# Windowed attention into a gated convolution block on one core: thirteen convolutions summed on GpSimd, the first batch's loads split by sequence, the work in a new order

## The chip, the cores and the metric

The kernel runs on one core of a Trainium2 chip. The core has five engines that matter here, each with its own queue that is worked off strictly in order: TensorE (PE; its weight loads are listed as PEld), VectorE (DVE), ScalarE (ACT), GpSimd (POOL), and SyncE (SP), which in this kernel issues all DMAs but one. An instruction that waits for another engine's result holds up everything behind it in its own queue. The metric is the device time of one execution in microseconds.

## The reference

Two stages follow each other. The first is attention over a symmetric window of 32 positions either way, the second a two-layer block whose hidden values are gated by their own three-tap convolution along the sequence:

```python
# q, k, v: (8 batches, 8 heads, 576 positions, 64), float32
scores = q @ k^T / 8
scores = where(|i - j| <= 32, scores, -1e9)
attn = softmax(scores); x = attn @ v            # heads put side by side: (8, 576, 512)
h = relu(x @ w_in)                              # (8, 576, 1024)
conv[s] = conv_w[0]*h[s-1] + conv_w[1]*h[s] + conv_w[2]*h[s+1]   # per channel, zero at both ends
out = (h * sigmoid(conv)) @ w_out               # (8, 576, 512), float32
```

## The kernel before, in words

All matrix work is done in bfloat16 with float32 sums in PSUM. The program is a flat list of steps in the string `ORDER` (line 29); the loop at its end (line 597) takes word by word and issues the step's instructions, so a word's place fixes the place of its instructions in each engine's queue. `name,args@bank` names a step, its arguments, and the PSUM bank (of eight) that it writes first. Nothing is reordered afterwards.

**Attention**, for batch b and half G of the heads (four heads on 4 x 32 partitions): `lq`/`lk` load q or k (576 KB each) into one of six staging tiles `st`; `cq`/`ck` cast them to bfloat16 (`qb`), on GpSimd (`p`) or ScalarE (`a`); `tq`/`tk` transpose them on VectorE into `qT`/`kT`. `sc,b,G,h` multiplies windows of 128 keys with 64 queries; h says which part of the nine 64-query tiles (the first four, 1024 columns, or the last five, 1280). `ex` is the exponential on ScalarE, `mk` multiplies by the 0/1 window mask (VectorE, `d`), `av` multiplies with v, `nr` divides by the row sums. v is loaded (`lv`), cast (`cv`) and copied once more with a shift of 64 rows (`vo`); both copies hold a column of ones for the row sums. `xp`/`xe` (TensorE and ScalarE) or `xt` (a transposing DMA) put the result with channels on the partitions, in `xT`.

**The block** runs over 12 chunks of 384 rows. The first two are split in halves, so there are 14 pieces P (0 to 3 are halves), each with four pairs m2 of 128-channel groups: 56 pairs. `ph,P,m2` is the first projection, `re` its ReLU into `hT`, `pc`/`tp` the convolution, `th` the tanh, `ga` the gate into `gT` (sigmoid by tanh). `py,c,i` is the second projection of 128 rows of chunk c, `ye` copies it from PSUM into one of four tiles `y`, `st` stores it (256 KB). The letter of a pair says who does the convolution:

- `P`: TensorE with diagonal weights `diag_w` of 128x128, 2 x 3 matmuls; the tanh is one instruction.
- `A`, `D`: TensorE with 64x64 quarters, 12 matmuls. The second group comes out with its halves exchanged: with `A` two ScalarE tanh of 64 partitions turn them back through `z`, with `D` two VectorE gates of 64 partitions do.
- `X`: ScalarE writes the first tap into PSUM (2 instructions), VectorE adds the other two (4), and no TensorE is used.

`cw` brings `conv_w` by a small matmul into `conv_w_sb`, `dg,m` makes `diag_w` for a group, `li`/`ci` and `lo`/`co` load and cast the two weight matrices in four parts each. `s0` to `s7` fill constants and borders.

Of the kernel before, what the change touches and what calls it, by code (L numbers as in the profile page):

```python
# [14 lines left out]

ORDER = """
lq,0,1 s3 s1 lq,0,0 s2 cw@0 lv,0,1 s5 s0 s7 lk,0,1 dg,4,d lk,0,0 lv,0,2 dg,2,d lv,0,3 dg,1,d cq,0,1,a lv,0,0 dg,7,d  # L30
lv,0,4 dg,6,d dg,0,d li,0 cq,0,0,p tq,0,1 li,2 cv,0,1,p dg,5,d tq,0,0 li,3 ck,0,1,p s4 tk,0,1 li,1 ck,0,0,p dg,3,d
sc,0,1,0@0 lk,1,0 cv,0,2,p sc,0,1,1@4 tk,0,0 ex,0,1,0 vo,0,1,p lq,1,0 ex,0,1,1 mk,0,1,0,d sc,0,0,0@0 lq,1,1 ex,0,0,0
cv,0,0,p sc,0,0,1@4 mk,0,1,1,d cv,0,3,a vo,0,0,d lk,1,1 cv,0,4,p ex,0,0,1 mk,0,0,0,d av,0,1,0@0 nr,0,1,0 vo,0,2,p
av,0,0,0@2 lv,1,1 nr,0,0,0 vo,0,3,d ci,0,p xp,0,1@0 lv,1,2 xp,0,0@1 xe,0,1,a mk,0,0,1,d av,0,1,1@2 xe,0,0,a nr,0,1,1
av,0,0,1@4 lv,1,0 ci,2,p ph,0,0@0 nr,0,0,1 ci,3,p ph,0,2@6 re,0,0 lo,2 pc,0,0,P@7 re,0,2 ci,1,p xp,0,3@4 th,0,0,P
xp,0,4@5 lo,3 xe,0,3,a ph,0,3@6 ga,0,0,P ck,1,0,p xe,0,4,a xp,0,2@4 re,0,3 ph,0,1@7 xe,0,2,a lo,1 cq,1,0,p tk,1,0
pc,0,3,P@5 re,0,1 ph,1,3@4 th,0,3,P tq,1,0 lk,2,1 cq,1,1,p pc,0,1,P@6 re,1,3 ph,2,0@7 th,0,1,P ga,0,3,P sc,1,0,0@0
re,2,0 lo,0 ck,1,1,p tq,1,1 ph,2,2@4 ex,1,0,0 ph,1,0@5 ga,0,1,P re,2,2 lv,1,3 cv,1,1,p sc,1,0,1@0 mk,1,0,0,d re,1,0
ph,2,3@4 ex,1,0,1 tk,1,1 lv,1,4 cv,1,2,p pc,0,2,P@5 ph,2,1@6 re,2,3 vo,1,1,d th,0,2,P lk,2,0 cv,1,0,p sc,1,1,0@0
re,2,1 ph,1,2@4 ga,0,2,P ex,1,1,0 mk,1,0,1,d pc,1,0,P@5 lq,2,0 co,2,p re,1,2 mk,1,1,0,d ph,1,1@6 th,1,0,P pc,1,2,P@4  # L40
vo,1,0,d re,1,1 lq,2,1 co,3,p sc,1,1,1@0 th,1,2,P ga,1,0,P pc,1,3,P@6 ex,1,1,1 ga,1,2,P pc,1,1,P@5 lk,3,0 co,1,p s6
pc,2,1,P@4 th,1,3,P mk,1,1,1,d av,1,1,0@0 th,1,1,P av,1,0,0@2 th,2,1,P lv,2,1 ck,2,1,p ga,1,1,P pc,2,0,P@7 nr,1,0,0
pc,2,3,P@5 th,2,0,P nr,1,1,0 pc,2,2,P@2 lq,3,0 co,0,p tk,2,1 xp,1,1@3 xp,1,0@0 xe,1,1,a py,0,0@1 lv,2,0 cv,1,3,p
xe,1,0,a ga,1,3,P ga,2,0,P th,2,2,P lk,4,0 vo,1,2,d cv,1,4,a py,0,2@0 ye,0,0,a vo,1,3,d th,2,3,P lv,2,2 ck,2,0,p
ga,2,1,P ph,3,2@1 ga,2,3,P ye,0,2,a ga,2,2,P ph,3,0@3 st,0,0 cq,2,0,p re,3,2 tk,2,0 av,1,1,1@4 re,3,0 av,1,0,1@6
nr,1,1,1 lk,3,1 cq,2,1,p py,1,0@0 nr,1,0,1 lq,3,1 ck,3,0,p ph,3,3@4 tq,2,1 ye,1,0,a xp,1,2@1 lv,2,3 cv,2,1,p re,3,3
pc,3,2,P@0 tq,2,0 xe,1,2,a sc,2,1,0@2 th,3,2,P ph,3,1@6 ex,2,1,0 st,1,0 ga,3,2,P cq,3,0,p xp,1,3@1 tk,3,0 pc,3,0,P@7
re,3,1 xe,1,3,a xp,1,4@4 lv,2,4 cv,2,0,p pc,3,3,P@5 th,3,0,P mk,2,1,0,d pc,3,1,P@6 xe,1,4,a vo,2,0,d sc,2,1,1@0 st,0,2
ck,4,0,p th,3,1,P py,0,1@4 ex,2,1,1 ga,3,1,P ga,3,0,P lq,4,0 tq,3,0 th,3,3,P cv,2,2,p lq,4,1 sc,2,0,0@0 ye,0,1,a
ph,4,0@6 vo,2,1,p ga,3,3,P ex,2,0,0 tk,4,0 st,0,1 sc,2,0,1@0 ck,3,1,p re,4,0 ph,4,2@4 mk,2,1,1,d ex,2,0,1 lv,3,1  # L50
mk,2,0,0,d cq,3,1,p pc,4,0,P@6 tk,3,1 re,4,2 lk,4,1 cv,2,3,p av,2,0,0@0 lv,3,0 th,4,0,P mk,2,0,1,d vo,2,2,p av,2,1,0@2
py,1,1@4 ga,4,0,P lk,5,1 cv,2,4,p tq,3,1 lv,3,2 ph,4,3@6 vo,2,3,p ye,1,1,a nr,2,0,0 lq,5,0 pc,4,2,A@4 nr,2,1,0 re,4,3
cq,4,0,p av,2,1,1@0 th,4,2,A lv,3,4 pc,4,3,A@2 nr,2,1,1 cq,4,1,p av,2,0,1@6 xt,2,0 th,4,3,A ga,4,2,A ph,4,1@0 cv,3,1,p
xt,2,1 nr,2,0,1 re,4,1 ga,4,3,A sc,3,0,0@4 ck,4,1,p xt,2,2 pc,4,1,P@0 ex,3,0,0 tq,4,0 cv,3,0,p sc,3,1,0@2 th,4,1,P
lv,3,3 mk,3,0,0,d py,1,2@6 vo,3,0,p ex,3,1,0 ga,4,1,P xt,2,3 mk,3,1,0,d py,2,1@7 ye,1,2,a cv,3,2,p xt,2,4 vo,3,1,d
cq,5,0,p sc,3,0,1@0 ye,2,1,a lk,5,0 av,3,1,0@4 tk,4,1 ex,3,0,1 py,2,2@6 st,1,1 cv,3,4,p nr,3,1,0 lv,4,0 ck,5,1,p
mk,3,0,1,d lv,4,1 av,3,0,0@4 sc,3,1,1@0 st,2,1 nr,3,0,0 py,2,0@7 ex,3,1,1 tq,5,0 xt,3,1 cv,3,3,p tq,4,1 vo,3,2,p
sc,4,0,0@0 ye,2,0,a ph,5,0@4 ex,4,0,0 xt,3,0 vo,3,3,d ph,5,2@0 ck,5,0,p re,5,0 st,1,2 mk,4,0,0,d ye,2,2,a lq,6,0
mk,3,1,1,d ph,5,3@2 lq,5,1 re,5,2 tk,5,0 st,2,2 cv,4,0,p av,3,0,1@0 re,5,3 av,3,1,1@4 nr,3,0,1 lv,4,2 cv,4,1,p
pc,5,2,D@6 st,2,0 vo,4,0,p pc,5,0,A@2 nr,3,1,1 th,5,2,D lv,4,4 ph,5,1@0 th,5,0,A lv,4,3 ga,5,2,D xt,3,3 ph,6,2@4  # L60
# [573 lines left out]
```

## Time and profile before

| | before |
|---|---|
| three runs | 225.03, 223.29, 221.05 us (median 223.29) |
| span of the profiled execution (the page gives no other time for it) | 221.8 us |
| VectorE, ScalarE, GpSimd busy | 190.1, 162.3, 94.2 us |
| moved by DMA | 45.96 MB, 207 GB/s over the span |
| granted TensorE clock | 1.000 |

Times in a profile are counted from the span's start. Nearly every instruction is issued through one helper, so line numbers say little here and the groups are told apart by what they write and read: `gT<-PS,hT` is a gate, `qb<-st` a cast of q or k, `PS<-hT,diag_w` a convolution on TensorE. A group's row gives its form, how many there are, the busy time of them together (overlaps counted once), the mean of one in ns, and the engine's idle time just before them with what ended it.

### The profile page before, as it was taken

The numbers are of one execution on the slowest core, as the hardware profiler recorded it, in microseconds if no ns is written. First come the engines' busy times: TensorE is split into PE (matmuls) and PEld (weight loads), VectorE is DVE, ScalarE is ACT, GpSimd is POOL, SyncE is SP. The second block draws the span as 40 slices with busy tenths as digits, with TensorE's granted clock in tenths as the row PEclk, the third lists the DMA queues.
The fourth block names the chain that finished last, engine by engine and source line by source line (L and its number), as shares of the span: only waits on it lengthen the run. The fifth ranks groups of instructions, "written<-read, shape, count | busy, mean of one in ns | idle before, by whom it ended". The sixth has DMA issues, their size and how long they took to land.

```text
span 221.8 us, 7235 instructions
## 1 busy us (share of the span) xinstructions
PE 192.9 (87%) x3026; PEld 114.5 (52%) x3026; DVE 190.1 (86%) x321; ACT 162.3 (73%) x260; POOL 94.2 (42%) x113
## 2 busy tenths in 40 slices
PE   1044999799999899899998999999999999999993
PEld 0033898657754445554554554564555455554441
...
GB/s 214 333 263 386 339 254 351 354 318 350 284 313 300 137 133 258 250 260 193 369 332 178 222 230 244 222 53 106 98 3 145 69 136 50 38 79 42 142 101 136
DMA packets 65348, 45.96 MB, mean 207 GB/s; under 512 B 53516, under 2 KB 55588, under 8 KB 65316
## 3 DMA queue, kind: packets, MB, share of 16 engines
...
## 4 chain that ended last, share of the span: by engine, by line
PE 41%; DVE 40%; ACT 9%; issue 4%; POOL 3%; DMA 1%; ACTq 0%; DVEq 0%; POOLq 0%
PE PS L175 41%; DVE gT L175 9%; DVE attn L175 6%; DVE xn L175 6%; DVE kT L175 5%; DVE vo L175 5%; DVE qT L175 4%; ACT hT L175 3%; ACT z L175 3%; DVE diag_w L175 2%; ACT attn L175 2%; POOL qb L175 2%; DVE PS L175 2%; ACT PS L175 2%; DMA conv_w<-in_moe_conv_w_dram 1%
## 5 line engine op out<-in xcount | busy, mean ns | idle before, releaser
L175 PE MATMUL PS<-xT,w_in_sb 128*128 128x385 bf16 (+3 forms) x448 | 71.4, 309 | 1.2 <-DVE xn L175 0.5
L175 PE MATMUL PS<-w_out_sb,gT 128*128 128x512 bf16 x288 | 66.7, 380 | 0.1
L175 PEld LDWEIGHTS <-w_in_sb 128*128 128x128 bf16 x448 | 41.5, 100 | 25.7 <-issue 5.2
L175 POOL TENSOR_SCALAR qb<-st 128x1152 bf16<-128x1152 f32 x31 | 37.6, 1214 | 40.2 <-issue 8.9
L175 ACT ACTIVATE hT<-PS 128x770 bf16<-128x770 f32 (+3 forms) x56 | 40.2, 721 | 11.8 <-PE PS L175 10.8
L175 ACT ACTIVATE attn<-PS 128x1024 bf16<-128x1024 f32 (+1 forms) x32 | 36.0, 1132 | 11.2 <-PE PS L175 11.2
L175 DVE SCALAR_TENSOR_TENSOR gT<-PS,hT 128x384 bf16<-128x384 f32 (+2 forms) x66 | 40.2, 617 | 4.2 <-ACT PS L175 3.4
L175 PEld LDWEIGHTS <-gT 128*128 128x128 bf16 x288 | 26.5, 98 | 30.2 <-issue 0.9
L175 ACT ACTIVATE PS<-PS 128x384 f32<-128x384 f32 (+1 forms) x56 | 31.9, 572 | 6.2 <-PE PS L175 5.0
L175 POOL TENSOR_SCALAR ve<-vst 128x512 bf16<-128x512 f32 x38 | 28.4, 754 | 15.5 <-PE PS L175 11.6
L175 DVE TENSOR_TENSOR attn<-attn,mask 128x1024 bf16<-128x1024 bf16 (+1 forms) x32 | 29.3, 923 | 6.2 <-ACT attn L175 6.0
L175 ACT COPY y<-PS 128x512 f32<-128x512 f32 x36 | 20.8, 585 | 17.7 <-PE PS L175 17.7
L175 PE MATMUL PS<-hT,diag_w 64*64 64x384 bf16 (+2 forms) x456 | 31.1, 311 | 2.8 <-DVE gT L175 1.2
L175 DVE TENSOR_TENSOR xn<-PS,rec 128x512 bf16<-128x512 f32 (+1 forms) x32 | 26.4, 824 | 1.4 <-DVE rec L175 0.3
L175 PE MATMUL PS<-qT,kT 32*128 32x64 bf16 x1152 | 15.4, 195 | 11.7 <-DVE kT L175 9.3
L175 ACT ACTIVATE z<-PS 64x384 f32<-64x384 f32 x48 | 23.3, 485 | 0.9
L175 PEld LDWEIGHTS <-diag_w 64*64 64x64 bf16 (+1 forms) x456 | 18.3, 104 | 10.2 <-issue 6.3
L175 PEld LDWEIGHTS <-kT 32*128 32x128 bf16 x1152 | 11.9, 96 | 20.1 <-DVE kT L175 10.2
L175 DVE SCALAR_TENSOR_TENSOR PS<-hT,conv_w_sb,PS 128x384 f32<-128x384 bf16 x36 | 19.6, 618 | 1.6 <-ACT PS L175 1.6
L175 DVE STREAM_TRANSPOSE kT<-qb 128x576 uint32<-128x576 uint32 x16 | 19.7, 1240 | 0.7 <-PE PS L175 0.7
L175 PE MATMUL PS<-ve,attn 128*64 128x65 bf16 x384 | 16.4, 203 | 3.8 <-DVE attn L175 2.2
L175 DVE STREAM_TRANSPOSE qT<-qb 128x576 uint32<-128x576 uint32 x16 | 19.6, 1244 | 0.0
...
## 6 DMA issues: line engine op xcount, KB each, us to landing
...
```

The source lines that it names most:

```text
L175: return lambda *args, **kwargs: tc.keep_in_program_order(do(*args, **kwargs))
```

## The change

- **First batch.** For batch 0, q and k of both G are loaded, cast and transposed in two parts along the sequence (q: rows 0 to 255, 256 KB, and the rest; k: rows 0 to 287, 288 KB, and the rest). That makes four loads, four casts and four transposes more.
- **Kind `G`.** Thirteen pairs get a fifth kind. `add_tap` multiplies on GpSimd each of the two groups with its tap's weight (two instructions of 384 columns, 192 in a half piece) into a float32 tile, for the second and third tap into `tap`, and then adds `tap` to `zg` (one instruction of 768 columns): six multiplications and two additions. The tanh reads `zg` (two buffers) and writes the PSUM bank that the gate reads. Three of the thirteen are in half pieces.
- **Other kinds.** `A` goes from 24 pairs to 11, `D` from 5 to 7, `X` from 9 to 9 (one of them in a half piece now), `P` in whole pieces from 2 to 4 and in half pieces from 16 to 12.
- **Masks.** Eight of the 32 `mk` go to GpSimd: two `affine_select` of 64 partitions each that write zeros outside the window.
- **Who copies.** `cq`/`ck` on GpSimd: 31 whole ones become 21 and 4 of the parts; on ScalarE 1 becomes 7 and 4 parts. `cv` on ScalarE: 2 becomes 18. `ci`/`co` on ScalarE: none becomes 3. `dg`: 5 of 8 go from VectorE to ScalarE (three instructions of 128 columns each). `ye`: 10 of 36 go from ScalarE to VectorE.
- **End.** The last projection tile `py,11,2`, its copy and its store are done in two halves of 256 columns.
- **Order.** The whole string `ORDER` is another one, with other banks, and with it every queue: the first word is now a k load, loads of a batch stand in blocks, and two parts of `w_in` (`li,1`, `li,2`) are loaded behind q and k of batch 1 instead of before them. `cw` and the copy behind it (`cc`) are two words.

```diff
 ORDER = """
-lq,0,1 s3 s1 lq,0,0 s2 cw@0 lv,0,1 s5 s0 s7 lk,0,1 dg,4,d lk,0,0 lv,0,2 dg,2,d lv,0,3 dg,1,d cq,0,1,a lv,0,0 dg,7,d
-lv,0,4 dg,6,d dg,0,d li,0 cq,0,0,p tq,0,1 li,2 cv,0,1,p dg,5,d tq,0,0 li,3 ck,0,1,p s4 tk,0,1 li,1 ck,0,0,p dg,3,d
-sc,0,1,0@0 lk,1,0 cv,0,2,p sc,0,1,1@4 tk,0,0 ex,0,1,0 vo,0,1,p lq,1,0 ex,0,1,1 mk,0,1,0,d sc,0,0,0@0 lq,1,1 ex,0,0,0
...
-ga,13,3,A st,10,0 py,11,0@0 ye,10,2,a st,10,2 py,11,1@1 ye,11,0,a st,11,0 py,11,2@0 ye,11,1,a st,11,1 ye,11,2,a
-st,11,2
+lk,0,0,1 s1 cw@0 cc dg,6,a dg,0,d dg,3,a s4 lq,0,1,0 cq,0,1,0,p s2 s5 dg,7,d dg,2,a lk,0,1,0 ck,0,1,0,p s0 lq,0,0,0
+cq,0,0,0,a ck,0,0,1,a tk,0,1,0 lk,0,0,0 ck,0,0,0,p tq,0,0,0 tq,0,1,0 sc,0,1,0@0 lk,0,1,1 lv,0,2 ck,0,1,1,p cv,0,2,p
+ex,0,1,0 dg,1,a lq,0,1,1 lv,0,1 cv,0,1,p cq,0,1,1,a tk,0,0,0 s3 s7 sc,0,0,0@3 tk,0,0,1 tk,0,1,1 ex,0,0,0 lv,0,0
+cv,0,0,a mk,0,1,0,d tq,0,1,1 vo,0,1,d vo,0,0,d lq,0,0,1 sc,0,1,1@4 cq,0,0,1,a ex,0,1,1 tq,0,0,1 mk,0,0,0,p lv,0,4
+lv,0,3 cv,0,3,a li,0 li,3 lk,1,0 av,0,0,0@2 nr,0,0,0 av,0,1,0@0 sc,0,0,1@4 ex,0,0,1 nr,0,1,0 cv,0,4,p vo,0,3,d
+vo,0,2,d xp,0,0@2 xp,0,1@0 ci,0,a xe,0,0,a xe,0,1,a mk,0,1,1,p ck,1,0,p av,0,1,1@5 mk,0,0,1,d av,0,0,1@3 nr,0,1,1
...
+pc,13,3,X@2 ph,13,1@6 pc,12,2,G tp,12,2,G re,13,1 ph,13,0@4 re,13,0 th,12,2,G@6 py,8,2@0 tp,13,3,X ph,13,2@4 ye,8,2,a
+th,13,3,X re,13,2 ga,12,2,G py,10,1@6 st,9,0 st,8,0 ye,9,1,d ga,13,3,X pc,13,1,X@4 pc,13,2,A@1 ye,10,1,a tp,13,1,X
+py,9,2@0 py,10,0@7 pc,13,0,G tp,13,0,G py,10,2@6 st,8,2 st,9,1 th,13,2,A ga,13,2,A ye,9,2,a th,13,1,X th,13,0,G@1
+ga,13,1,X ye,10,0,a ye,10,2,a st,9,2 st,10,0 st,10,1 st,10,2 ga,13,0,G py,11,1@0 ye,11,1,a st,11,1 py,11,0@2 ye,11,0,a
+st,11,0 py,11,2,0@0 ye,11,2,0,a st,11,2,0 py,11,2,1@3 ye,11,2,1,a st,11,2,1
 """
+    zg_ = tiles(2, [128, 2, CH], FP32, "zg")
+    tap = tiles(1, [128, 2, CH], FP32, "tap")[0]
...
+    def part_of(y, part):
+        if not part:
+            return 0, RP
+        first = (256, 288)[y] // 32
+        return (0, first) if part[0] == 0 else (32 * first, RP - first)
...
     def mk(b, G, h, e):
         attn, n = attn_of(b, G, h)
-        {"d": vector, "p": gpsimd}[e].tensor_tensor(out=attn, in0=attn, in1=mask[:, 0:4 * n], op=ALU.mult)
+        if e == "d":
+            vector.tensor_tensor(out=attn, in0=attn, in1=mask[:, 0:4 * n], op=ALU.mult)
+            return
+        for lo, sign in ((0, 1), (64, -1)):
+            part = attn[lo:lo + 64].rearrange("p (t x) -> p t x", x=64)
+            gpsimd.affine_select(
+                out=part, in_=part, compare_op=ALU.is_ge, fill=0.0, base=0,
+                pattern=[[0, n // 16], [-sign, 64]], channel_multiplier=sign,
+            )
...
+    def add_tap(P, m2, kk):
+        z = where["zg", P, m2]
+        to = (tap if kk else z)[:, :, 0:width(P)]
+        for i in range(2):
+            m = 2 * m2 + i
+            gpsimd.tensor_scalar(
+                out=like(to[:, i, :], P), in0=taps(P, m, kk), scalar1=conv_w_sb[:, kk, m:m + 1],
+                scalar2=0.0, op0=ALU.mult, op1=ALU.add,
+            )
+        if kk:
+            z = z[:, :, 0:width(P)]
+            gpsimd.tensor_tensor(out=z, in0=z, in1=to, op=ALU.add)
...
+        if kind == "G":
+            where["pc", P, m2] = bank
+            scalar.activation(
+                conv_out(P, m2), where["zg", P, m2][:, :, 0:width(P)], AF.Tanh, bias=0.0, scale=1.0
+            )
+            return
```

194 lines of the change are left out of this document (110 added, 84 removed).

## The prediction

> **What bounds the kernel now.** First the span and busy times, then the same by stretch, then the chain of waits at both ends.
>
> ```profile
> span 221.8 us, 7235 instructions
> PE 192.9 (87%) x3026; PEld 114.5 (52%) x3026; DVE 190.1 (86%) x321; ACT 162.3 (73%) x260; POOL 94.2 (42%) x113
> ```
>
> ```profile
> core 0: us, PE busy (x) PEld busy (x) DVE busy (x) ACT busy (x) POOL busy (x), PEclk, DMA share, GB/s
> 0.00:24.48 24.48, 7.20 (x234) 5.99 (x234) 20.42 (x46) 8.22 (x9) 17.82 (x26) 1.00 1.01 310
> 24.48:75.00 50.52, 46.81 (x829) 34.78 (x829) 46.68 (x71) 36.28 (x65) 34.90 (x39) 1.00 1.08 305
> 75.00:120.00 45.00, 42.03 (x706) 22.94 (x698) 43.35 (x67) 35.21 (x55) 23.95 (x26) 1.00 1.02 243
> 120.00:160.00 40.00, 39.64 (x606) 20.78 (x604) 34.59 (x62) 32.51 (x51) 17.52 (x24) 1.00 0.73 171
> 160.00:200.00 40.00, 39.21 (x572) 21.71 (x571) 34.23 (x63) 35.91 (x57) 0.00 (x0) 1.00 0.30 76
> 200.00:222.00 22.00, 18.05 (x106) 8.28 (x104) 10.87 (x18) 14.21 (x25) 0.00 (x0) 0.99 0.26 99
> ```
>
> TensorE is idle 28.9 us: 17.3 before the first projection, 6.7 from there to 120 us, where VectorE has 90.0 of 95.5 us busy and is the bound, 1.1 to 200 us, where TensorE is the bound, and about 4 at the end. GpSimd does nothing after 160 us. The clock is full throughout and plays no part.
>
> ```profile
> 4.46 3.84 DVE diag_w L175 x6
> ...
> 13.16 0.64 PE PS L175 x29
> ...
> 200.29 17.82 PE PS L175 x104
> 218.13 0.58 ACT y L175
> ```
>
> In the chain of waits (start, length, what) the first scores come at 13.16 us, behind six `diag_w` on VectorE; the end is TensorE without a gap, then one copy and its store.
>
> **The start.** Loads and GpSimd's and TensorE's first work, from the timeline:
>
> ```profile
> 0.81 0.87 SPq L175 DMA_DIRECT2D st<-in_q_dram  x2
> 4.89 1.15 ACT L175 CAST qb<-st 128x1152 bf16<-128x1152 f32 x1 [2.16 <-DMA st<-in_q_dram]
> 6.55 1.35 POOL L175 TENSOR_SCALAR qb<-st 128x1152 bf16<-128x1152 f32 x1 [2.65 <-DMA st<-in_q_dram]
> 9.02 1.15 POOL L175 TENSOR_SCALAR qb<-st 128x1152 bf16<-128x1152 f32 x1 [0.24 <-DMA st<-in_k_dram]
> 11.74 0.62 POOL L175 TENSOR_SCALAR ve<-vst 128x512 bf16<-128x512 f32 x1
> 24.49 2.77 PE L175 MATMUL PS<-xT,w_in_sb 128*128 128x193 bf16 x16
> 85.92 4.09 PE L175 MATMUL PS<-xT,w_in_sb 128*128 128x385 bf16 x24
> 209.29 8.81 PE L175 MATMUL PS<-w_out_sb,gT 128*128 128x512 bf16 x40
> ```
>
> A 576 KB load takes 1.66 us of the stream (6.55 − 4.89) behind a fixed 2.4 us. The parts that the first scores need (third load in the queue) so land near 0.81 + 2.4 + 832/576 x 1.66 = 5.6 us; the GpSimd cast of a part, by 1152 and 512 columns (1.15 and 0.62 us) 0.65 us, ends at 6.3. VectorE has two `diag_w` (0.64 each) ahead of three part transposes instead of seven among whole ones. ScalarE makes three `diag_w` first and casts q's other part behind them, near 7.3 us, and VectorE transposes that part before the one needed. Scores: about 8.6 us, 4.5 earlier. From there ScalarE carries more than before: four exponentials, one `diag_w`, two part casts, two v casts, two `xe` and one weight cast, about 11 us by the rows below, against 11.3 us in the trace before (13.16 to 24.49). The next scores share bank 3 with the first and wait for their exponential (1.0 us); all of batch 0's later attention is queued behind on TensorE, and ScalarE fills the time with casts. First projection: near 20.3 us. I take −4.2. Bounds: 0, if the loads for it are late (below), and −4.5. The four more loads cost SyncE 0.43 us each (0.87 for two), hidden behind the transfers.
>
> **TensorE's share.** The groups by form:
>
> ```profile
> L175 PE MATMUL PS<-hT,diag_w 64*64 64x384 bf16 x348 | 18.8, 328 | 1.5 <-ACT hT L175 1.1 <-ACT PS L175 0.2
> L175 PE MATMUL PS<-hT,diag_w 128*128 128x192 bf16 x96 | 10.1, 246 | 1.3 <-DVE gT L175 1.2
> L175 PE MATMUL PS<-hT,diag_w 128*128 128x384 bf16 x12 | 2.3, 326 | 0.0
> L175 ACT ACTIVATE z<-PS 64x384 f32<-64x384 f32 x48 | 23.3, 485 | 0.9
> L175 ACT ACTIVATE PS<-PS 128x384 f32<-128x384 f32 x40 | 19.3, 482 | 3.7 <-PE PS L175 3.2
> L175 ACT ACTIVATE PS<-PS 128x768 f32<-128x768 f32 x16 | 12.8, 797 | 2.5 <-PE PS L175 1.8 <-DVE PS L175 0.4
> L175 ACT ACTIVATE PS<-hT,conv_w_sb 128x384 f32<-128x384 bf16 x18 | 9.7, 574 | 0.3
> L175 ACT COPY y<-PS 128x512 f32<-128x512 f32 x36 | 20.8, 585 | 17.7 <-PE PS L175 17.7
> L175 ACT CAST ve<-vst 128x512 bf16<-128x512 f32 x2 | 1.2, 624 | 0.0
> L175 DVE SCALAR_TENSOR_TENSOR gT<-PS,hT 128x384 bf16<-128x384 f32 x45 | 24.3, 549 | 3.4 <-ACT PS L175 3.1
> L175 DVE SCALAR_TENSOR_TENSOR gT<-z,hT 128x384 bf16<-128x384 f32 x24 | 16.4, 684 | 1.4 <-ACT z L175 1.2
> L175 DVE SCALAR_TENSOR_TENSOR gT<-PS,hT 128x768 bf16<-128x768 f32 x11 | 10.5, 952 | 0.6 <-ACT PS L175 0.3
> L175 DVE SCALAR_TENSOR_TENSOR gT<-PS,hT 64x384 bf16<-64x384 f32 x10 | 5.5, 555 | 0.2
> L175 DVE SCALAR_TENSOR_TENSOR PS<-hT,conv_w_sb,PS 128x384 f32<-128x384 bf16 x36 | 19.6, 618 | 1.6 <-ACT PS L175 1.6
> L175 POOL TENSOR_SCALAR qb<-st 128x1152 bf16<-128x1152 f32 x31 | 37.6, 1214 | 40.2 <-issue 8.9 <-DMA st<-in_q_dram 8.6 <-DVE qT L175 8.4
> L175 POOL TENSOR_SCALAR ve<-vst 128x512 bf16<-128x512 f32 x38 | 28.4, 754 | 15.5 <-PE PS L175 11.6 <-DMA vst<-in_v_dram 3.5
> masks.py:199 POOL TENSOR_SCALAR_AFFINE_SELECT ident<-ident 128x128 bf16<-128x128 bf16 x1 | 0.3, 292 | 0.1
> ```
>
> An `A` or `D` pair costs TensorE only 18.8/29 = 0.65 us, a half `P` 10.1/16 = 0.63, a whole `P` 1.15. Eleven `A`/`D` and four half `P` fewer, two whole `P` more: −7.1 − 2.5 + 2.3 = −7.3 us. By piece, 4.7 of it lies in pieces 1 to 7, 2.6 in pieces 8 to 13. The first part runs where VectorE is the bound, so VectorE's sum decides there.
>
> **VectorE.** Gates and taps: an `A` costs 0.55 + 0.68, `D` 0.55 + 2 x 0.56, whole `P` and `G` 0.95, half `P` and `G` 0.55, `X` 4 x 0.62 + 0.95. −13 `A`, +2 `D`, +2 whole and −4 half `P`, +10 whole and +3 half `G`, one `X` into a half piece: −3 us. Five `diag_w` at 0.64: −3.2. Eight masks at about 0.9: −7.2. Ten copies of 512 columns from PSUM, scaled from the 384-column gate to some 0.7: +7; at 0.585, as on ScalarE, +6. Together −6, and most of that in the start and the last third: from the first projection to piece 7 only two masks leave and four copies come. Against it stands a wait on GpSimd, seen in one row at two times:
>
> ```profile
> L175 DVE TENSOR_TENSOR attn<-attn,mask 128x1024 bf16<-128x1024 bf16 x14 | 12.7, 909 | 3.5 <-ACT attn L175 3.4
> ...
> L175 DVE TENSOR_TENSOR attn<-attn,mask 128x1024 bf16<-128x1024 bf16 x2 | 1.4, 686 | 0.5 <-ACT attn L175 0.5
> ```
>
> The first is before 160 us, with GpSimd 59% busy (94.2/160), the second after, with GpSimd idle: 0.22 us more per instruction. With GpSimd 78% busy to the end it would be 0.3 on some 70 masks, shifted v copies and gates from `z`: +3 us or so over the kernel. I take −1 us for the stretch from the first projection to 120 us (from 0 to −4), and nothing for VectorE behind it.
>
> **ScalarE.** Pairs: −13 `A` (0.48 + 2 x 0.485), and the others by their tanh: −9. Casts: 6 whole (1.15), 4 parts (0.65), 16 of v (0.62), 3 of weights (about 1.05), 15 instructions of `diag_w` (0.27 by the slope from 384 to 768 columns): +27. Nine copies `y`, halves counted: −6. Sum +12, so 174 of about 214: hidden beside VectorE and TensorE, and at the start already counted. Without that cover it costs up to 12.
>
> **GpSimd.** The trace has no `G` pair and no large `affine_select`. A multiplication of 384 columns, by the slope above, is 0.51 us. The addition of 768 columns with two inputs lies between one such stream, 0.83, and two, 1.66; I take two, because it reads two float32 tiles. A whole pair is 6 x 0.51 + 2 x 1.66 = 6.4 us (4.7 to 7.8, the upper end by the mean of the v casts, 754, over their undisturbed 620), a half one 4.2. A mask, from 0.29 us for 128 columns with the same slope, is 2.1 to 2.5. So: +64 + 13 (pairs), +18 (masks), −9 (ten q/k casts, four parts back), −12 (16 v casts), −3 (weights), +1: 94 becomes 166. From piece 5 on it is nine pairs, 13 casts of q or k, 11 of v, ten shifted copies and five masks, about 107 us. Before, piece 5 to TensorE's end is 85.92 to 218.1 us; less 3, and less what must follow the last pair (three tiles at 1.76, tanh 0.8, gate 0.95) and what precedes the first, 120 us are there. It fits, with 13 to spare. Each tanh of a `G` pair sits in ScalarE's queue: if the sum is late, the copies `ye` behind it wait, and TensorE for their banks. For the last pair (13,0), TensorE has five tiles, one projection and one convolution, 5 x 1.76 + 1.36 + 0.65 = 10.8 us, as cover after the projection, and GpSimd 6.4 plus what is left of pair (12,2); I add +1 us.
>
> **The end.** The last tile's second half starts 0.9 us earlier relative to its store: copy and store of 128 KB instead of 256 KB behind the last matmul. −0.7 (0 to −1; the same eight weights are loaded twice).
>
> Sum: 221.8 − 4.2 − 1.0 − 2.6 + 1.0 − 0.7 = 214.3 against the profile's span, whose own time the page doesn't give; the median of the runs is 1.5 above the span, so **215.8 us**.
>
> **Rivals.**
> *GpSimd becomes the bound from piece 5 on.* Above 7.9 us a pair ((120 − 50)/9), the queue of sums is longer than TensorE's work, and each 0.1 us adds 0.9: at 8.5 us 221, at 9.5 us 230, slower than before. It decides from 7.9 us. For it: both engines already lengthen each other (909 to 686 above, 754 to 620), and `z` gates and masks would now meet GpSimd after 160 us too. Against: fewer such VectorE instructions (71 for 94), and 13 us of room. The Trainium skill (SBUF — State Buffer, section "Who interferes with whom") says that a VectorE instruction with two SBUF inputs and a GpSimd instruction that reads SBUF exclude one another for a whole instruction. The trace agrees as far as 909 against 686 ns go. By that rule this rival is the likelier the longer GpSimd's instructions get.
> *The earlier start is lost.* The DMA share is 1.01 to 1.08 up to 75 us; 4.2 us at 305 GB/s are 1.3 MB that would have to come sooner, or VectorE, 94% busy, doesn't take it up. 215.8 + 4.2 = 220. Against: part of the loads wait for free staging tiles, not for the stream.
> *The addition costs one stream and VectorE sheds its 4 us.* 215.8 − 1 − 3 − 1 = 210.8.
>
> **Chances.** The measurement tells 2% from no change: 218.8 to 227.8 us is "within". The forecast (212 to 218.8) 0.47, the cheap addition 0.08: faster 0.55. The lost start 0.16 and GpSimd's milder half 0.11: within 0.27. GpSimd above 9.2 us a pair: 0.18. The range for 8 in 10 goes from 209 (a little under the cheap case) to 227, leaving out the slow tail; the forecast's own range is 212 to 219.
>
> **What would show it.** First scores near 8.6 us and the first projection near 20.3 in the timeline; the `zg` additions at 1.66 us each, and GpSimd near 166 us; VectorE still over 90% from the first projection to piece 7; masks and `z` gates after 160 us over 0.8 us. I am wrong if ScalarE's tanh from `zg` waits on GpSimd for more than a few us in all, or TensorE's idle time behind 120 us exceeds 4 us.

## The result, and the profile after

The changed kernel takes 248.18 us (median of four runs, 246.74 to 249.33) against 223.54 us before (four runs, 221.05 to 225.03): the ratio is 1.112, with a 95% interval of 1.103 to 1.121. It is 24.6 us slower, where 7.5 us faster was forecast, and 21 us above the range. The profile of the head-by-head run below is of its longest execution (241.42 us at a granted clock of 0.972, where the other three have 0.977 to 0.993).

The head of the page of the kernel after, and its busy times by the same stretches as before (us of the span, length; then PE, PEld, DVE, ACT, POOL busy; granted clock, DMA share, GB/s):

```profile
span 245.0 us, 7039 instructions
PE 190.6 (78%) x2890; PEld 111.7 (46%) x2890; DVE 195.8 (80%) x311; ACT 172.0 (70%) x269; POOL 179.3 (73%) x210
```

```profile
0.00:24.48 24.48, 1.82 (x66) 1.50 (x66) 7.07 (x29) 7.10 (x16) 5.37 (x15) 1.00 0.34 108
24.48:75.00 50.52, 37.98 (x756) 30.09 (x757) 42.09 (x67) 38.89 (x68) 37.53 (x49) 1.00 0.98 271
75.00:120.00 45.00, 39.16 (x582) 21.27 (x572) 41.51 (x60) 32.13 (x43) 38.21 (x41) 0.96 0.85 199
120.00:160.00 40.00, 34.36 (x508) 18.00 (x507) 37.87 (x53) 29.54 (x45) 36.25 (x40) 0.96 0.84 234
160.00:200.00 40.00, 38.11 (x702) 20.62 (x700) 36.78 (x59) 32.71 (x50) 32.02 (x34) 1.00 0.68 172
200.00:245.00 45.00, 39.14 (x300) 20.25 (x292) 30.44 (x47) 31.65 (x50) 29.95 (x34) 1.00 0.32 97
```

Two things stand out. In the first stretch no engine is busy for a third of the time, and the DMA engines are not either: share 0.34 and 108 GB/s, where the kernel before had 1.01 and 310. And GpSimd is busy for 179.3 us (166 had been forecast), and VectorE for 195.8 us with ten instructions fewer, although by the prediction's count 6 us of its work had gone to other engines.

Where the loss arises is best seen from the start of the ReLUs of each piece (first ReLU of the piece, us from the span's start, read from the timelines; the last column is the span):

| | piece 0 | piece 5 | piece 8 | piece 13 | span |
|---|---|---|---|---|---|
| before | 26.0 | 87.4 | 129.4 | 199.4 | 221.8 |
| after | 40.0 | 99.9 | 152.1 | 221.7 | 245.0 |
| difference | +14.0 | +12.5 | +22.7 | +22.3 | +23.2 |

Some 14 us are lost ahead of the first ReLU, some 10 more between pieces 5 and 8, and next to nothing behind piece 8, where a gain had been forecast.

**The start.** The timeline of after (start, length, instruction; in brackets the idle time before and what ended it):

```profile
3.49 5.04 SPq L165 DMA_DIRECT2D st<-in_k_dram  x2
9.23 0.62 POOL L165 TENSOR_SCALAR qb<-st 128x512 bf16<-128x512 f32 x1 [7.86 <-DMA st<-in_q_dram]
...
16.80 0.61 PE L165 MATMUL PS<-qT,kT 32*128 32x64 bf16 x32 [13.76 <-DVE qT L165]
...
38.54 2.08 PE L165 MATMUL PS<-xT,w_in_sb 128*128 128x193 bf16 x16
```

and the DMA view of its first 22 us (busy share of the 16 DMA engines in 40 slices, and GB/s):

```profile
DMA  0000221222222222222223992222222223993232
GB/s 0 0 0 22 46 67 50 88 101 101 106 93 104 104 104 99 109 105 101 101 97 122 273 244 76 99 99 105 113 101 101 101 101 122 254 242 71 73 83 106
```

The share stands at two tenths and the rate at 100 GB/s while part loads run, with nine tenths and 250 GB/s for moments only (a v load was issued shortly before each). The parts are loaded with the four heads as the outermost dimension of the transfer (`[[S*D, 4], [g*D, 32], [1, g*D]]`). A whole load needs no such dimension, since its 4 x 32 rows lie at even distances and fold into one dimension of 128. The rate is about a quarter of the 400 GB/s at which the kernel before loads at its best in the same time. SyncE also sits on the issues: two of them take 5.04 us, where two whole ones took 0.87. The Trainium skill (DMA: Bandwidth & Descriptors, section "Rules for kernel authors") says that an outermost dimension smaller than 16 confines a DMA to that many engines; the trace agrees with 0.2 of the share, near the quarter that four of sixteen would be. The third load, which was to land at 5.6 us, was there for its cast at 12.14 us, and the fourth, whose transpose stands ahead in VectorE's queue, at 15.00. So the first scores came at 16.80 us and not at 8.6, and the first projection at 38.5 and not at 20.3; the last part of q landed only at 31.3.

**GpSimd and VectorE.** The groups by form (busy us, mean ns of one | idle before them):

```profile
L165 POOL TENSOR_TENSOR zg<-zg,tap 128x768 f32<-128x768 f32 x20 | 36.8, 1841 | 1.7
L165 DVE COPY vo<-ve 64x520 bf16<-64x520 bf16 x36 | 24.4, 678 | 0.9
L165 POOL TENSOR_SCALAR tap<-hT,conv_w_sb 128x384 f32<-128x384 bf16 x40 | 23.4, 598 | 0.9
L165 POOL TENSOR_SCALAR zg<-hT,conv_w_sb 128x384 f32<-128x384 bf16 x20 | 13.2, 671 | 7.8 <-ACT hT L165 7.6
L165 POOL TENSOR_SCALAR_AFFINE_SELECT attn<-attn 64x1280 bf16<-64x1280 bf16 x8 | 11.1, 1384 | 0.9 <-ACT attn L165 0.6
L165 DVE SCALAR_TENSOR_TENSOR gT<-z,hT 128x384 bf16<-128x384 f32 x11 | 9.9, 902 | 0.0
```

and the rows of the waits (engine, its output, what it waited for: us in all, times, longest):

```profile
POOL zg L165 <- ACT hT L165: 10.3, 5, 3.4
...
ACT PS L165 <- POOL zg L165: 4.3, 5, 2.0
```

A whole `G` pair takes 2 x 0.671 + 4 x 0.598 + 2 x 1.841 = 7.4 us. ScalarE's tanh waited for a sum only 4.3 us in all. Yet GpSimd is on the chain that ended last for 22% of the span, where it was 3% before:

```profile
DVE 26%; PE 26%; POOL 22%; SPq 9%; DMA 5%; issue 5%; ACT 5%; POOLq 0%; DVEq 0%; ACTq 0%
```

And the shifted v copies on VectorE take 678 ns instead of 437, and the gates from `z` 902 instead of 684. One place in the timeline of after shows how that reaches TensorE:

```profile
103.64 2.45 POOL L165 TENSOR_TENSOR zg<-zg,tap 128x768 f32<-128x768 f32 x1
104.46 2.46 DVE L165 COPY vo<-ve 64x520 bf16<-64x520 bf16 x2
106.97 0.19 PE L165 MATMUL PS<-vo,attn 128*64 128x65 bf16 x1 [1.81 <-DVE vo L165]
```

Two copies that take 0.3 us each where GpSimd is idle end 2.46 us after the first started, beside one addition (2.45 us, where the mean is 1.84) and its successor, and TensorE idles 1.81 us for them.

### The profile page after: what moved, and what is told of

Same layout as the page of the kernel before. It is cut to its first block, busy times and chain, and to the rows that moved or that the text cites. A ratio compares the mean times of both kernels' runs of the same rounds, so it can differ in the third digit from the quotient of the medians.

```text
span 245.0 us, 7039 instructions
## 1 busy us (share of the span) xinstructions
PE 190.6 (78%) x2890; PEld 111.7 (46%) x2890; DVE 195.8 (80%) x311; ACT 172.0 (70%) x269; POOL 179.3 (73%) x210
## 4 chain that ended last, share of the span: by engine, by line
DVE 26%; PE 26%; POOL 22%; SPq 9%; DMA 5%; issue 5%; ACT 5%; POOLq 0%; DVEq 0%; ACTq 0%
PE PS L165 26%; POOL zg L165 10%; SPq L165 9%; DVE gT L165 6%; DVE vo L165 6%; POOL tap L165 5%; DVE attn L165 4%; DMA st<-in_q_dram 4%; DVE xn L165 3%; DVE kT L165 2%; POOL attn L165 2%; ACT PS L165 2%; POOL qb L165 2%; POOL vo L165 2%; DMA xT<-xn 2%
## 5 line engine op out<-in xcount | busy, mean ns | idle before, releaser
L165 PE MATMUL PS<-w_out_sb,gT 128*128 128x512 bf16 (+1 forms) x296 | 67.1, 374 | 2.4 <-DVE gT L165 1.7
L165 ACT ACTIVATE hT<-PS 128x770 bf16<-128x770 f32 (+3 forms) x56 | 39.8, 720 | 12.6 <-PE PS L165 12.1
L165 POOL TENSOR_TENSOR zg<-zg,tap 128x768 f32<-128x768 f32 (+1 forms) x26 | 43.1, 1658 | 2.2
L165 POOL TENSOR_SCALAR qb<-st 128x1152 bf16<-128x1152 f32 (+2 forms) x25 | 28.6, 1153 | 19.1 <-DMA st<-in_k_dram 10.3
L165 PEld LDWEIGHTS <-kT 32*128 32x128 bf16 x1152 | 12.5, 96 | 39.6 <-issue 14.6
L165 DVE STREAM_TRANSPOSE kT<-qb 128x576 uint32<-128x576 uint32 (+1 forms) x18 | 19.9, 1121 | 12.2 <-POOL qb L165 12.2
L165 POOL TENSOR_SCALAR tap<-hT,conv_w_sb 128x384 f32<-128x384 bf16 (+1 forms) x52 | 28.8, 565 | 1.0
L165 DVE STREAM_TRANSPOSE qT<-qb 128x576 uint32<-128x576 uint32 (+2 forms) x18 | 20.0, 1118 | 7.1 <-ACT qb L165 7.1
L165 DVE COPY vo<-ve 64x520 bf16<-64x520 bf16 x36 | 24.4, 678 | 0.9
L165 POOL TENSOR_SCALAR ve<-vst 128x512 bf16<-128x512 f32 x22 | 15.6, 717 | 12.0 <-DMA vst<-in_v_dram 11.6
L165 POOL TENSOR_SCALAR_AFFINE_SELECT attn<-attn 64x1024 bf16<-64x1024 bf16 (+1 forms) x16 | 20.3, 1270 | 5.4 <-ACT attn L165 4.8
L165 POOL TENSOR_SCALAR zg<-hT,conv_w_sb 128x384 f32<-128x384 bf16 (+1 forms) x26 | 16.0, 627 | 10.6 <-ACT hT L165 10.3
```

Source lines behind the costliest of these rows:

```text
L165: return lambda *args, **kwargs: tc.keep_in_program_order(do(*args, **kwargs))
```

## The experiments

Of each run, the first ReLUs of pieces 0 and 8 are given where they matter. A run with a single time was executed once; it is set beside the median of the kernel before on the same chip, whose seven times there lie within 2 to 3 us of each other.

### The part loads, head by head

The kernel after with each part load as four DMAs of one head, so that 32 partitions are outermost:

```diff
-        sync.dma_start(to, bass.AP(src.tensor, src.offset, [[S * D, 4], [g * D, 32], [1, g * D]]))
+        for a in range(4):
+            sync.dma_start(
+                to[32 * a:32 * a + 32],
+                bass.AP(src.tensor, src.offset + a * S * D, [[g * D, 32], [1, g * D]]),
+            )
```

> The changed kernel, with each part load of batch 0 issued as four DMAs of one head each (32 partitions outermost) instead of one DMA whose source runs over 4 heads outermost; the same bytes, the same order. Theory 1 (a part load whose outermost step is 4 runs on few of the 16 DMA engines: 108 GB/s and a DMA share of 0.34 before 24.48 us): the share goes to about 1, SyncE needs some 1.7 us of issue per part, the first scores come near 10 us instead of 16.8, the first projection near 24 instead of 37.7, all later pieces 12 to 15 us earlier, time 232 to 236. Theory 2 (the start does not matter because GpSimd's sums set the time): below 5 us, 243 or more. Theory 3 (runs of 2 KB instead of 4.5 KB slow the stream): share and start as in the changed kernel.

238.49 us (237.55 to 241.42), ratio 1.064 (1.056 to 1.072), beside 224.39 for the kernel before: 9.7 us less than the changed kernel, and a loss of 14.1 us instead of 24.6. That is theory 1, but short of its 232 to 236 us. Windows and timeline of this kernel:

```profile
0.00:24.48 24.48, 4.83 (x180) 3.88 (x180) 13.49 (x39) 12.12 (x23) 10.63 (x21) 1.00 0.76 188
```

```profile
0.81 1.79 SPq L165 DMA_DIRECT2D st<-in_k_dram  x4
...
11.49 0.61 PE L165 MATMUL PS<-qT,kT 32*128 32x64 bf16 x32 [8.33 <-DVE qT L165]
...
28.24 2.77 PE L165 MATMUL PS<-xT,w_in_sb 128*128 128x193 bf16 x16
```

The share doubles to 0.76. It doesn't reach 1.01; four issues take SyncE 1.79 us for 288 KB, and parts issued one behind the other at that pace come to 165 GB/s (288 x 1024 bytes in 1.79 us). Scores now come at 11.5 us, earlier than the 13.2 of before, and the first projection at 28.2 instead of 38.5 us, still 3.8 us later than before. So the start has a second fault, behind the scores.

### The same loads in the kernel before

The kernel before with only the loads of the first batch's q and k split as in the change (four heads outermost), and their transposes in two parts:

```diff
+        if b == 0:
+            f = (8, 9)[y]
+            for t0, g in ((0, f), (32 * f, RP - f)):
+                src = (q, k)[y][b, 4 * G:4 * G + 4, t0:t0 + 32 * g, :]
+                sync.dma_start(
+                    st_[slot(y, b, G) % NST][:, 2 * t0:2 * t0 + 64 * g],
+                    bass.AP(src.tensor, src.offset, [[S * D, 4], [g * D, 32], [1, g * D]]),
+                )
+            return
```

> The kernel before with this one part of the change: each q and k load of batch 0 in two parts with 4 heads outermost, transposed in two parts, casts whole, order and all else as before. Theory 1: eight parts at about 108 GB/s take 2.36 MB / 0.108 = 22 us instead of 6.5, so the first projection moves from 24.5 to 36 to 40 us and the time from 223 to 235 to 240. Theory 3 and any theory that puts the loss on the new order alone: 228 or less.

239.51 us beside 224.39, at the upper end of what was expected; the first projection came at 41.3 us, a little later than the 36 to 40. Its windows and its first scores:

```profile
0.00:24.48 24.48, 0.77 (x18) 0.68 (x22) 8.16 (x33) 2.43 (x2) 5.40 (x13) 1.00 0.31 105
```

```profile
24.30 1.25 PE L175 MATMUL PS<-qT,kT 32*128 32x64 bf16 x72 [21.17 <-DVE kT L175]
```

Again 0.31 and 105 GB/s: the shape of the load does it, in another kernel and another order. The head-by-head loads move the same short rows at 0.76, so the length of the rows is not the cause.

### One tap instead of three

Two runs in which the `G` pairs compute only the first tap on GpSimd; the second and third, with their additions, are left out of the convolution. One has the loads of the change, the other the head-by-head loads.

```diff
-            add_tap(P, m2, 1)
...
-            add_tap(P, m2, 2)
```

> The changed kernel, where a pair of kind G computes only its first tap on GpSimd (two instructions instead of eight; the second and third tap are left out). Loads as in the changed kernel. Theory A (GpSimd's 7.4 us per pair made the 10 us that pieces 5 to 7 lose after the start): GpSimd's busy time falls from 179 to about 100 us, pieces 0 to 4 stay as they are, piece 7 comes at 120 to 123 instead of 132.3, time 236 to 240. Theory B (the order and VectorE's load make it, GpSimd only runs beside them): 244 or more.

> Both edits: loads by head, and only the first tap of a G pair on GpSimd (the second and third left out). If theories 1 and A hold and the two costs add: 248 - 13 - 10 = 222 to 227. If GpSimd had only filled the hole that the late loads made: near e1.

234.96 us (below the 236 to 240 expected) and 223.81 us, beside 224.39 for the kernel before. The taps are worth 13.2 us by the first run and 14.7 by the second. With both edits the kernel is back at the time of before, though not at the 215.8 us forecast, and with part of the work left out. The page and two groups of the second kernel:

```profile
PE 185.9 (84%) x2867; PEld 111.6 (50%) x2890; DVE 183.6 (83%) x311; ACT 172.0 (77%) x269; POOL 105.1 (47%) x132
```

```profile
L165 DVE COPY vo<-ve 64x520 bf16<-64x520 bf16 x36 | 18.8, 521 | 1.6 <-POOL ve L165 0.8
...
L165 DVE SCALAR_TENSOR_TENSOR gT<-z,hT 128x384 bf16<-128x384 f32 x11 | 6.9, 630 | 0.0
```

Not an instruction of VectorE has changed against the head-by-head run, yet it is busy 13.5 us less (183.6 for 197.1), nearly as much as the time fell (14.7). Copies and gates account for 9 us of it: 36 x (660 − 521) and 11 x (990 − 630) ns (660 and 990 are their means in the head-by-head run); the masks, 12 of each size, for another 4 (from 1043 and 972 to 901 and 774 ns). In the pair with the loads of the change the share is smaller: VectorE falls from 195.8 to 187.1 us, 8.7, and the time by 13.2. Piece 8 starts at 131.9 us instead of 145.2.

### The tanh freed from the sums

Head-by-head loads, and the tanh of a `G` pair reads the hidden values instead of the sum, which GpSimd still computes and nobody uses:

```diff
-                conv_out(P, m2), where["zg", P, m2][:, :, 0:width(P)], AF.Tanh, bias=0.0, scale=1.0
+                like(conv_out(P, m2), P), taps(P, (2 * m2, 2 * m2 + 1), 1), AF.Tanh, bias=0.0, scale=1.0
```

> Loads by head as in e1. All sums of the G pairs run on GpSimd as before, but the tanh of a G pair reads the hidden values and not the sums (the convolution of these pairs is left out of the result), so that nobody waits for a sum. Theory A1 (the loss is tanh and gate waiting for late sums): 226 or less, near the run with one tap. Theory A2 (the loss is GpSimd's queue itself: casts, v copies and masks of later batches stand behind the sums, and VectorE is locked out by them): within 3 us of e1, 235 to 239.

236.76 us beside 223.41 (ratio 1.060, inside the interval of the head-by-head run). By this one execution, waiting for the sums is worth 1.7 us. GpSimd's part of the chain that ended last falls to 5%, from 23% in the head-by-head run, and VectorE's rises from 21 to 35%:

```profile
DVE 35%; PE 32%; ACT 8%; SPq 7%; issue 6%; POOL 5%; DMA 5%; DVEq 0%; ACTq 0%; POOLq 0%
```

So that GpSimd's sums arrive too late, the rival of the prediction, costs little by itself: without that wait, VectorE (194.2 us busy) holds the kernel at nearly the same time.

### Memsets of the same length

Head-by-head loads, and the eight GpSimd instructions of a pair replaced by memsets of together about the same length, so that the queue is nearly as full (173.8 us busy for 179.0) but the instructions read nothing; the convolution of these pairs is left out.

```diff
-            gpsimd.tensor_scalar(
-                out=like(to[:, i, :], P), in0=taps(P, m, kk), scalar1=conv_w_sb[:, kk, m:m + 1],
-                scalar2=0.0, op0=ALU.mult, op1=ALU.add,
-            )
+            gpsimd.memset(to.rearrange("p y x -> p (y x)")[:, 0:576 if full else 420], 0.0)
...
-            gpsimd.tensor_tensor(out=z, in0=z, in1=to, op=ALU.add)
+            for n in (768, 768, 384) if full else (768, 128):
+                gpsimd.memset(z.rearrange("p y x -> p (y x)")[:, 0:n], 0.0)
```

> Loads by head as in e1. The eight instructions of a G pair are replaced on GpSimd by memsets of about the same length together, 7 us (they read nothing; the convolution of these pairs is left out), with the same waits and readers. Theory L (GpSimd's reads exclude VectorE's two-input instructions): masks on VectorE fall from about 1.0 us to 0.8, gates from z from 0.99 to 0.6, VectorE's busy time from 197 to 188 or less, time 229 to 233. Theory Q (the queue: GpSimd is simply full and what stands behind the sums is late): VectorE may fall, the time stays at 235 or more.

228.77 us beside 223.41, just under the 229 to 233 of theory L. The groups of this kernel:

```profile
L165 DVE COPY vo<-ve 64x520 bf16<-64x520 bf16 x36 | 22.2, 617 | 1.2 <-POOL ve L165 0.4
...
L165 DVE SCALAR_TENSOR_TENSOR gT<-z,hT 128x384 bf16<-128x384 f32 x11 | 6.8, 620 | 0.0
```

About 10 of the 14.7 us are gone, and VectorE is busy 190.1 us instead of 197.1 (188 or less was expected). The two-input gates are back to 620 ns, the copies only to 617. But the run takes away a second thing: a memset doesn't wait for the hidden values. In the head-by-head run GpSimd stands 15.2 us in all waiting for ReLUs, with the casts of later batches behind it in its queue; here it waits for none. The row in the head-by-head run:

```profile
POOL zg L165 <- ACT hT L165: 15.2, 6, 5.5
```

No run here tells how much of the 10 us is the lengthening of VectorE and how much this queue, nor what the remaining 5 us are.

### The middle pairs back on TensorE

Head-by-head loads; the eight `G` pairs of pieces 1 to 7 become `P` (half pieces) or `A`, issued at the place of their tanh; five `G` pairs remain in the tail.

```diff
+        if kind == "G" and P < 8:
+            kind = "P" if P < 4 else "A"
+            pc(P, m2, kind, bank)
```

> Loads by head as in e1. The eight G pairs of pieces 1 to 7 are computed on TensorE again (kind P in half pieces, A in whole ones, at the place of their tanh), the five of pieces 8 to 13 stay on GpSimd. Nothing is left out. If the loss sits where GpSimd also has the casts and v copies of later batches (e1 against the run with one tap: 3 us at piece 3, 13 at piece 8, then no more than 2): 226 to 229, with piece 8 first at 132 to 135. If the tail's pairs cost as much each as the middle's: 232 or more.

233.79 us (232.49 to 235.46), ratio 1.047 (1.040 to 1.055): it missed the 226 to 229 and lies where the expectation put pairs of the tail that cost as much as those of the middle. By the pieces they cost half as much each: from piece 8 to the end the kernel takes 94.2 us where the one with a single tap takes 90.1, 4.1 us for five pairs, and ahead of piece 8 the eight pairs cost 13.3 (145.2 for 131.9). Of these only 7.5 us come back (piece 8 at 137.7). The likely reason for the rest is not tested: an order planned around `G` has the convolution where its result is due, so that TensorE computes it late, and ScalarE and VectorE get their share of `A` back (175.3 us busy for 172.1; 191.4 for 197.1, where one tap gave 183.6).

### Whole loads for the first batch as well

The last kernel with the first batch's q and k loaded whole, the half needed first in front, and the start reordered to suit:

```diff
-lk,0,0,1 s1 cw@0 cc dg,6,a dg,0,d dg,3,a s4 lq,0,1,0 cq,0,1,0,p s2 s5 dg,7,d dg,2,a lk,0,1,0 ck,0,1,0,p s0 lq,0,0,0
...
+lk,0,1 s1 lq,0,1 cw@0 cc dg,6,a lk,0,0 dg,0,d dg,3,a s4 lq,0,0 s2 s5 dg,7,d ck,0,1,p cq,0,1,a tk,0,1 tq,0,1 s0
+sc,0,1,0@0 sc,0,1,1@4 dg,2,a lv,0,2 ck,0,0,p ex,0,1,0 cq,0,0,p lv,0,1 lv,0,0 tk,0,0 ex,0,1,1 s3 s7 cv,0,2,p mk,0,1,0,d
...
```

> As e7, and batch 0's q and k are loaded, cast and transposed whole again, with the 128 partitions outermost, G = 1 first, and the first scores behind two loads and two diag_w on VectorE. From rows: loads land at 4.9 and 6.5 us, first scores near 9 to 9.5, the four exponentials done by 16, the first projection at 18.5 to 21. If the start is worth what the prediction said (4 us against before's 24.5, 8 against e1's 28.3): 218 to 221, faster than before. If what follows takes the gain up (VectorE or DMA bound from there): 224 or more.

235.4 us (235.15 to 235.66), ratio 1.054 (1.050 to 1.058): also missed, and instructive. Its timeline:

```profile
9.78 1.15 PE L164 MATMUL PS<-qT,kT 32*128 32x64 bf16 x72 [5.84 <-DVE qT L164]
...
15.06 0.59 DVE L164 COPY vo<-ve 64x520 bf16<-64x520 bf16 x2
...
21.85 4.53 DVE L164 COPY vo<-ve 64x520 bf16<-64x520 bf16 x4
22.77 4.61 POOL L164 TENSOR_SCALAR qb<-st 128x1152 bf16<-128x1152 f32 x4
...
28.91 1.31 PE L164 MATMUL PS<-xT,w_in_sb 128*128 128x193 bf16 x7
```

Whole loads gave scores at 9.8 us, better than the parts in any shape; but the first projection came at 28.9. Ahead of it stand four v copies of 0.29 us each (two took 0.59 at 15.06 us), and they took 4.53 us, beside the end of a mask on GpSimd and four casts run back to back: about one copy got through for each cast of 1.15 us.

### The masks alone

The kernel before with the eight masks of the change on GpSimd (each `mk` of that list with two `affine_select`) and nothing else moved:

```diff
-cv,0,0,p sc,0,0,1@4 mk,0,1,1,d cv,0,3,a vo,0,0,d lk,1,1 cv,0,4,p ex,0,0,1 mk,0,0,0,d av,0,1,0@0 nr,0,1,0 vo,0,2,p
+cv,0,0,p sc,0,0,1@4 mk,0,1,1,p cv,0,3,a vo,0,0,d lk,1,1 cv,0,4,p ex,0,0,1 mk,0,0,0,p av,0,1,0@0 nr,0,1,0 vo,0,2,p
```

> The kernel before with its eight masks of the change on GpSimd (two affine selections each) and nothing else moved. Theory L (a GpSimd instruction lengthens VectorE's two-byte copies and multiplications beside it, and the order waits for the masks): VectorE loses 8 masks of 0.9 us from its queue, but the weighted sums behind a mask wait 1.5 us longer each, and the copies beside the selections grow: 223 to 226 us. Rival M (VectorE is the bound and gets 7 us of room): 219 to 221 us.

228.95 us (227.85 to 230.65), ratio 1.024 (1.018 to 1.030): slower than either theory had it. Its timeline:

```profile
16.26 2.85 POOL L175 TENSOR_SCALAR_AFFINE_SELECT attn<-attn 64x1280 bf16<-64x1280 bf16 x2 [1.02 <-ACT attn L175]
...
19.77 2.35 POOL L175 TENSOR_SCALAR_AFFINE_SELECT attn<-attn 64x1024 bf16<-64x1024 bf16 x2
...
22.17 0.26 PE L175 MATMUL PS<-ve,attn 128*64 128x65 bf16 x1 [4.26 <-POOL attn L175]
...
28.26 1.96 PE L175 MATMUL PS<-xT,w_in_sb 128*128 128x193 bf16 x11
```

The two masks of the first batch take 5.2 us of GpSimd one behind the other, and TensorE stands 4.26 us before the weighted sums that need the second; what VectorE and TensorE have queued behind those sums slides with them, and the first projection goes from 24.49 to 28.26 us. Of the 5.4 us lost by the medians (4.3 between the two profiles), 3.8 are there at the first ReLU (29.8 for 26.0); piece 8 is 3.5 late, piece 13 4.3. So the other six masks cost little, and bring nothing, though VectorE is busy 185.8 us instead of 190.1.

### The first batch's masks back, in the change's own order

> The change with head-by-head loads, and the first batch's two masks (0,0,0 and 0,1,1) back on VectorE; all else stays. Theory M (in the change's own order, too, the two masks hold up the start, as they did alone in the kernel before, where they moved the first ReLU by 3.8 us): first projection 24.5 to 26 us instead of 28.24, and 235 to 236.5 us. Theory Q (here the second half's exponentials wait for the q parts cast on ScalarE, and the weight casts and the xT copies stand behind them in ScalarE's queue, so the masks have cover): first projection 27.5 to 28.3 us, and 237.5 to 239 us.

```diff
-cv,0,0,a mk,0,1,0,d tq,0,1,1 vo,0,1,d vo,0,0,d lq,0,0,1 sc,0,1,1@4 cq,0,0,1,a ex,0,1,1 tq,0,0,1 mk,0,0,0,p lv,0,4
+cv,0,0,a mk,0,1,0,d tq,0,1,1 vo,0,1,d vo,0,0,d lq,0,0,1 sc,0,1,1@4 cq,0,0,1,a ex,0,1,1 tq,0,0,1 mk,0,0,0,d lv,0,4
...
-vo,0,2,d xp,0,0@2 xp,0,1@0 ci,0,a xe,0,0,a xe,0,1,a mk,0,1,1,p ck,1,0,p av,0,1,1@5 mk,0,0,1,d av,0,0,1@3 nr,0,1,1
+vo,0,2,d xp,0,0@2 xp,0,1@0 ci,0,a xe,0,0,a xe,0,1,a mk,0,1,1,d ck,1,0,p av,0,1,1@5 mk,0,0,1,d av,0,0,1@3 nr,0,1,1
```

239.21 us (238.72 to 239.64), ratio 1.074 (1.067 to 1.082), no better than the head-by-head run, and just beyond the range of theory Q. Theory M is out; of theory Q the masks' cover holds, its account of the path only in part:

```profile
20.45 0.72 ACT L165 CAST qb<-st 128x640 bf16<-128x640 f32 x1 [0.85 <-DMA st<-in_q_dram]
...
22.54 0.26 PE L165 MATMUL PS<-ve,attn 128*64 128x65 bf16 x1 [3.23 <-DVE attn L165]
...
23.56 0.72 PE L165 MATMUL PS<-qT,kT 32*128 32x64 bf16 x40
...
27.13 0.26 PE L165 MATMUL PS<-ve,attn 128*64 128x65 bf16 x1 [1.25 <-DVE attn L165]
...
28.67 2.51 PE L165 MATMUL PS<-xT,w_in_sb 128*128 128x193 bf16 x16
```

The last q part lands only at 20.45 us, behind some 17 us of issues on SyncE. From there the chain goes over its cast on ScalarE (0.72 us), its transpose and a mask on VectorE, weighted sums, four v copies and another mask on VectorE, and the last weighted sums (27.13), which the projection follows without a gap. So in this order the late parts cover the masks, and then VectorE holds up TensorE. The weight casts on ScalarE are not on this path: the columns of the first projection were cast by 26.50 us.

### The kernel before with a reordered start

The kernel before, with its whole loads in another order (k and q of the half needed first in front), five of the eight `dg` on ScalarE, and the last projection tile in two column halves; nothing of the convolution or the masks goes to GpSimd.

```diff
-lq,0,1 s3 s1 lq,0,0 s2 cw@0 lv,0,1 s5 s0 s7 lk,0,1 dg,4,d lk,0,0 lv,0,2 dg,2,d lv,0,3 dg,1,d cq,0,1,a lv,0,0 dg,7,d
-lv,0,4 dg,6,d dg,0,d li,0 cq,0,0,p tq,0,1 li,2 cv,0,1,p dg,5,d tq,0,0 li,3 ck,0,1,p s4 tk,0,1 li,1 ck,0,0,p dg,3,d
...
+lk,0,1 s1 lq,0,1 s3 s2 cw@0 lq,0,0 s5 s0 s7 lk,0,0 lv,0,1 s4 dg,4,a dg,0,d dg,1,d lv,0,2 lv,0,3 ck,0,1,p cq,0,1,a
+tk,0,1 lv,0,0 tq,0,1 lv,0,4 li,0 dg,5,a li,2 dg,2,a li,3 li,1 cq,0,0,p cv,0,1,p ck,0,0,p dg,3,d tq,0,0 sc,0,1,0@0
...
```

> The kernel before with whole loads, k of the first transposed group ahead of q, five of the eight diagonal expansions on ScalarE instead of VectorE, and the last projection tile in two column halves; no GpSimd convolution and no GpSimd masks. Theory S (what the start of the change was after can be had without splitting the loads: first scores come when one k and one q transfer of full width have landed, and every later milestone moves with the first projection): first scores at 9.8 us as in the run with whole loads and the middle on TensorE, first projection at 21 to 22 us, 219.5 to 221 us in all. Rival T (the order from 26 us on is bound by VectorE, which gives the gain at the start back before 130 us): first projection early, the eighth piece at 129 us as before, 222.5 to 223.5 us.

222.82 us (220.73 to 224.13, twelve runs), ratio 0.995 (0.991 to 0.999): faster than before by half a per cent, with the interval just clear of one but far below the 2% that count as a change here. Two lines of its start and one from behind piece 5:

```profile
9.61 1.15 PE L175 MATMUL PS<-qT,kT 32*128 32x64 bf16 x72 [5.04 <-DVE qT L175]
...
22.86 0.34 PE L175 MATMUL PS<-xT,w_in_sb 128*128 128x193 bf16 x1
...
88.52 0.58 ACT L175 COPY y<-PS 128x512 f32<-128x512 f32 x1 [2.26 <-DMA out_dram<-y]
```

The scores are 3.6 us earlier, the first ReLU 2.1 (23.9 for 26.0), and piece 5 still 2.0. At piece 6 it is 0.7, at piece 7 0.5, and piece 8 begins 0.7 us later than before. The time is that of rival T, but its reason, VectorE, isn't what the trace shows. Most of the gain goes between the starts of pieces 5 and 6, where VectorE is busy 7.8 of 10.2 us (8.7 of 8.9 before). There ScalarE, with the next ReLUs behind it in its queue, waits 2.26 us for a tile `y` until a store has landed; before, the same copy began without a wait, at 88.15 us. The 0.7 us between the medians are as much as the column halves at the end were to bring; no run here separates the two.

## Why the prediction was wrong, point by point

- **The start, −4.2 (bounds 0 to −4.5).** It came out as +14.0 at the first ReLU. The step that failed is the landing of the parts that the first scores need, put at 5.6 us: it priced a part by its bytes at the rate of a whole load (1.66 us for 576 KB). The transfer's outermost dimension went from 128 rows to 4 heads, and with it the rate to about a quarter; the third load was there at 12.1 us. Undoing that alone gains 9.7 us, and the same loads in the kernel before cost 15.1 (executed once). The upper bound of 0 was given only for late weight loads, and no rival priced the shape, though the kernel's code shows it. The rule cited above in the Trainium skill speaks against this very edit.
- **First projection "near 20.3".** It would have failed with fast loads too. With scores at 11.5 (head by head) and 9.8 us (whole), the projection still came at 28.2 and 28.9. The step added up ScalarE's work between scores and projection, about 11 us. In the traces ScalarE isn't what holds the stretch: the chain goes over late loads (v at 18.2 us and q at 20.45 in the two head-by-head runs), masks, and above all v copies on VectorE that wait out GpSimd's instructions (3.47 us for four in the head-by-head run, 4.53 with whole loads).
- **VectorE, −1 to 120 us, with "+3 us or so over the kernel" for what GpSimd does to it.** The mechanism was named, and the size was off by four. From before to after the v copies grew by 36 x (678 − 437), the `z` gates by 11 x (902 − 684) and the masks by about 24 x 60 ns: 8.7 + 2.4 + 1.4 = 12.5 us. The estimate took 0.22 us from the masks and scaled it with GpSimd's busy share to 0.3 for some 70 instructions. The masks grew least (0.06 us on top of before), the copies most (0.24); and the busy share isn't all that counts, since memsets with nearly the same share left VectorE 7.0 us less busy. That the lengthening goes with the taps is shown: leaving two out takes 8.7 and 13.5 us off VectorE in the two pairs, and 13.2 and 14.7 off the time; the memsets take 7.0 and about 10. That it is the larger part of those 13 to 15 us is the likely reading, not a shown one, because each of these runs also relieves GpSimd's queue; the run with the tanh freed speaks for it, the chain's 22% on GpSimd in the kernel after against it.
- **TensorE's share behind piece 8, −2.6.** Perhaps right, and hidden. From the first ReLU of piece 8 to the end, before takes 92.4 us and after 92.9; the run with one tap takes 90.1, which is −2.3, about what this step, the end and the +1.0 for GpSimd sum to; the other run with one tap, 90.3, agrees. Both leave out work that the step counted on GpSimd, so the runs allow the step and don't show it.
- **GpSimd, +1.0, rival "bound from piece 5 on".** The additions were taken at 1.66 us and measured 1.84, a pair 7.4 instead of 6.4 us, the masks 2.3 and 2.8 instead of 2.1 to 2.5. That is under the rival's deciding 7.9 us, and freeing the tanh gained 1.7 us. The rival that ended on the slower side thus had the wrong mechanism in the main; its own sentence on the Trainium skill (SBUF — State Buffer, section "Who interferes with whom") had the right one, a lock that lengthens VectorE, but it was used to weigh the rival's chance and not priced for itself.
- **ScalarE and the end.** ScalarE came to 172.0 us for the 174 forecast, with `dg` at 0.39 us an instruction instead of 0.27. That it was hidden behind the other engines is borne out by the chain, 5% ScalarE in the kernel after. The last copy is 256 columns and takes 0.37 us instead of 0.58; what that is worth in the time no run shows alone.
- **What would show it.** Of the signs named, TensorE's idle time behind 120 us answered: 5.6 + 1.9 + 5.9 = 13.4 us by the windows, where more than 4 was to mean "wrong"; but the kernel before has 5.1 us by the same windows, so the sign was set too low. VectorE is busy 91% from the first projection to piece 7, as forecast, and that says nothing against the change. ScalarE's wait for sums, 4.3 us, was the sign that pointed the wrong way.
